# Block-causal attention with a gated convolution FFN: another static instruction order, other PSUM banks, other fill matmuls

## The chip, the cores and the metric

The kernel runs on one core of one Trainium2 chip. A time is the device time of one execution in microseconds (us). The five engines are TensorE (PE, with its weight loads as PEld), VectorE (DVE), ScalarE (ACT), GpSimd (POOL) and SyncE (SP, which here only issues transfers).

## The reference

The mask is by blocks of 64 positions; the scores are taken with q and k of 8 batches, 8 heads, 576 positions and 64 elements a head. The output of the attention goes through a two-layer network with a convolution of three taps as a gate.

```python
scores = scale * np.matmul(q, k.transpose(0, 1, 3, 2))
mask = block_i >= block_j                       # blocks of 64
scores = np.where(mask, scores, -1000000000.0)
attn = softmax(scores)                          # with 1e-09 added to the sum
x = (attn @ v).transpose(0, 2, 1, 3).reshape(8, 576, 512)
h = np.maximum(x @ w_in, 0.0)                   # 512 -> 1024
conv_out = sum(conv_w[k] * hp[:, k:k + S, :] for k in range(3))
return (h * sigmoid(conv_out)) @ w_out          # 1024 -> 512
```

## The kernel before

The work is written as 4,929 small operations, each for one engine, in a list (`Plan`, whose method `op` records them). For each there is a function that issues its instructions. `follow` then issues them in the order of a table of numbers, `ORDER`; each engine runs its own instructions in that order and waits by semaphores for what it needs from the others. Two more tables go with it: `BANKS` gives each accumulator the one of the eight PSUM banks that it lives in, and `FILLS` names operations ahead of which some matmuls without use are issued (line L1204: 128x512 matmuls into a bank that nobody holds at that moment; `32:0:12` means ahead of operation 32, into bank 0, 12 matmuls).

The attention goes by pairs of heads. For the first batch a pair is visited twice: part A is blocks 0 to 3, part B blocks 4 to 8; all later pairs are one visit. Of a visit these steps matter here, with their lines:

- loads: `qkf` (L564), `qT`, `kT` (L535), `vn` (L548), `vxa` (L574); the weights, 64-bit numbers, are `gh`, `gl` (w_in, L722) and `x` (w_out, L750). SP issues all of them, but for the first k tile and two pieces of w_in, which ACT issues.
- part A alone: PE transposes q and k (L800), ACT copies them out of PSUM (L508).
- scores: PE, L867, `banks<-kT,qT`; DVE takes the maxima (L879), PE exchanges them between halves (L888, or POOL and ACT by L503 and L842), DVE combines them (L902); ACT takes the exponentials with their sums (L911, `p`).
- DVE transposes the probabilities (L979) into `pta` (part A, two buffers) or `ptw` (all others, a single buffer); PE multiplies them by v (L990).
- DVE scales the result (L1001), ACT and POOL split it in a high and a low part (L1005, L1009).

The network of a half of a batch (`ffn`) follows when its four pairs are done: per 128 of the 1024 channels 12 matmuls (L1043), then ACT and DVE in turn (L1057, L1060, L1064, L1068, L1073, L1076, L1080) and POOL (L1083); then the products with w_out, 24 matmuls a tile (L1109), whose result ACT takes out of PSUM (L1117, `stage`) and SP stores (L1120). At the start ACT, DVE and POOL also take the weights apart into two 32-bit halves (L586 to L630), with three matmuls and one ACT copy for each piece (L685, L688, L691, L697).

Each PSUM bank is held from the first matmul that writes it to the last instruction that reads it; a PE instruction that opens a bank waits for the last reader before.

Of the kernel before, what the change touches and what calls it, by code (L numbers as in the profile page):

```python
# [184 lines left out]
"""  # L185

FILLS = """
32:0:12 30:0:13 64:0:2 69:1:2 126:0:7 235:6:4 512:2:1 250:0:6 532:0:2 390:7:3 813:0:2 4909:0:3
"""


# [1048 lines left out]
```

## Time and profile before

| | |
|---|---|
| runs shown | 670.77, 671.48 (median), 672.11 us |
| the profiled execution's own time | 671.29 us |
| its span (first to last instruction) | 669.4 us |
| busy, share of the span | PE 97%, PEld 81%, DVE 84%, ACT 80%, POOL 47% |
| granted clock of TensorE | 1.000 |
| L1204 matmuls (fills) | 57 |

The span leaves out 1.9 us of the profiled execution. A busy PE is not a PE at its peak: matmuls are pipelined, and each is shown longer than the distance to the next.

### The profile page before, as it was taken

The numbers are of one execution on the slowest core, as the hardware profiler recorded it, in microseconds if no ns is written. First come the engines' busy times: TensorE is split into PE (matmuls) and PEld (weight loads), VectorE is DVE, ScalarE is ACT, GpSimd is POOL, SyncE is SP. The second block draws the span as 40 slices with busy tenths as digits, with TensorE's granted clock in tenths as the row PEclk, the third lists the DMA queues.
The fourth block names the chain that finished last, engine by engine and source line by source line (L and its number), as shares of the span: only waits on it lengthen the run. The fifth ranks groups of instructions, "written<-read, shape, count | busy, mean of one in ns | idle before, by whom it ended". The sixth has DMA issues, their size and how long they took to land.

```text
span 669.4 us, 24942 instructions
## 1 busy us (share of the span) xinstructions
PE 652.0 (97%) x9734; PEld 544.0 (81%) x9734; DVE 560.4 (84%) x1333; ACT 537.1 (80%) x1989; POOL 315.1 (47%) x651
## 2 busy tenths in 40 slices
PE   8888999999999999999999999999999999999997
PEld 6666678768888788788888798888879798799986
DVE  3998889998999889997989779997899869995641
ACT  5998879967989786897888778997888787895643
POOL 0454455654356524446355534555555515444421
PEclk9999999999999999999999999999999999999999
DMA  7996752355454353425333442542353451230001
GB/s 176 194 215 143 145 104 50 70 105 91 73 104 96 64 97 78 99 44 103 74 72 72 97 96 41 117 90 43 75 99 79 93 92 43 48 87 1 17 32 63
DMA packets 238521, 58.26 MB, mean 87 GB/s; under 512 B 228524, under 2 KB 232900, under 8 KB 238404
## 3 DMA queue, kind: packets, MB, share of 16 engines
q1 hardware_dynamic: 237060, 55.76, 41.6%
q8 instruction: 76, 1.25, 0.8%
q10 hardware_dynamic: 1344, 0.92, 0.5%
q14 instruction: 41, 0.34, 0.2%
HBM read 47.21 MB, written 9.44 MB: 85 GB/s over the span
## 4 chain that ended last, share of the span: by engine, by line
PE 74%; DVE 4%; ACT 3%; issue 1%; POOL 0%; ACTq 0%; POOLq 0%; DVEq 0%
PE banks L1109 27%; PE banks L1043 27%; PE banks L867 11%; PE banks L990 10%; ACT p L911 1%; DVE st L879 1%; DVE ptw L979 1%; DVE t L1064 1%; DVE t L1076 1%; DVE t L1068 0%; ACT gh L1080 0%; ACT t L1073 0%; DVE rb L961 0%; DVE kT L820 0%; ACT t L1060 0%
## 5 line engine op out<-in xcount | busy, mean ns | idle before, releaser
L911 ACT ACTIVATE p<-banks,st 128x160 f32<-128x160 f32 (+8 forms) x576 | 220.9, 401 | 22.2 <-DVE st L902 20.4
L1043 PE MATMUL banks<-x,wih 128*128 128x290 f32 (+3 forms) x1024 | 185.1, 300 | 0.5 <-ACT p L911 0.4
L1043 PEld LDWEIGHTS banks<-x,wih 128*128 128x128 f32 x1024 | 154.2, 188 | 10.9 <-issue 4.5
L1083 POOL TENSOR_TENSOR gl<-t,gh 128x289 fp32r<-128x289 f32 (+3 forms) x128 | 106.1, 839 | 97.0 <-ACT gh L1080 82.4
L979 DVE STREAM_TRANSPOSE ptw<-p 128x448 f32<-128x448 f32 (+8 forms) x272 | 128.7, 498 | 13.5 <-ACT p L911 7.0
L879 DVE TENSOR_REDUCE st<-banks 128x2 f32<-128x320 f32 (+7 forms) x288 | 125.5, 472 | 11.0 <-PE banks L867 9.9
L503 POOL TENSOR_SCALAR st<-st 32x4 f32<-32x4 f32 (+2 forms) x280 | 67.7, 242 | 122.7 <-DVE st L879 50.5
L911 ACT ACTIVATION_READ_ACCUMULATOR p<-banks,st 128x1 f32 x576 | 122.8, 213 | 0.0
L1109 PE MATMUL banks<-woh,gh 128*128 128x512 f32 (+1 forms) x296 | 118.0, 399 | 0.3 <-ACT stage L1117 0.3
L1109 PE MATMUL banks<-woh,gl 128*128 128x512 f32 (+1 forms) x296 | 115.3, 390 | 0.2 <-POOL gl L1083 0.2
L1109 PE MATMUL banks<-wol,gh 128*128 128x512 f32 (+1 forms) x296 | 115.3, 390 | 0.0
L1043 PE MATMUL banks<-x,wil 128*128 128x290 f32 (+3 forms) x512 | 105.7, 299 | 0.0
L867 PE MATMUL banks<-kT,qT 64*32 64x96 f32 (+8 forms) x4464 | 100.0, 302 | 1.5 <-DVE rb L1001 0.6
L1064 DVE SCALAR_TENSOR_TENSOR t<-h,cw,t 128x289 f32<-128x289 f32 (+3 forms) x128 | 70.8, 558 | 29.0 <-ACT t L1060 28.4
L867 PEld LDWEIGHTS banks<-kT,qT 64*32 64x32 f32 x4464 | 69.7, 105 | 23.5 <-issue 4.1
L990 PEld LDWEIGHTS banks<-ptw,vn 64*64 64x64 f32 x2304 | 72.3, 133 | 20.0 <-issue 4.7
L990 PE MATMUL banks<-ptw,vn 64*64 64x160 f32 (+8 forms) x2304 | 85.2, 297 | 2.5 <-issue 1.4
L1043 PEld LDWEIGHTS banks<-x,wil 128*128 128x128 f32 x512 | 81.6, 188 | 4.3 <-issue 2.5
L1060 ACT ACTIVATE t<-h,cw 128x289 f32<-128x289 f32 (+3 forms) x128 | 68.0, 539 | 6.3 <-POOL gl L1083 2.0
L1068 DVE SCALAR_TENSOR_TENSOR t<-h,cw,t 128x288 f32<-128x288 f32 (+3 forms) x128 | 69.8, 555 | 1.4
L1073 ACT ACTIVATE t<-t 128x289 f32<-128x289 f32 (+3 forms) x128 | 55.1, 447 | 18.9 <-DVE t L1068 18.3
L1076 DVE SCALAR_TENSOR_TENSOR t<-t,h 128x289 f32<-128x289 f32 (+3 forms) x128 | 63.4, 503 | 7.6 <-ACT t L1073 6.9
(105 smaller groups left out, 812.9 us busy)
## 6 DMA issues: line engine op xcount, KB each, us to landing
vn<-in_v_dram SPq DMA_DIRECT2D x128, 144.0 KB, 3.6
out_dram<-stage SPq DMA_DIRECT2D x35, 256.0 KB, 2.6
qT<-in_q_dram SPq DMA_DIRECT2D x112, 72.0 KB, 3.2
kT<-in_k_dram SPq DMA_DIRECT2D x112, 72.0 KB, 3.1
x<-in_moe_w_out_dram SPq DMA_DIRECT2D x8, 512.0 KB, 5.2
gl<-in_moe_w_in_dram SPq DMA_DIRECT2D x4, 512.0 KB, 6.7
vxa<-in_v_dram SPq DMA_DIRECT2D x8, 128.0 KB, 5.4
gh<-in_moe_w_in_dram SPq DMA_DIRECT2D x2, 512.0 KB
```

The source lines that it names most:

```text
L867: nc.tensor.matmul(both(sb)[32 * quad:32 * quad + 32, h, o:o + w].rearrange("p (u n) -> p u n", n=32), t["q"].ap[r, 64 * b + 32 * g:64 * b ...
L879: nc.vector.tensor_reduce(out=st.ap[:, 0, c, :], in_=both(sb)[:, :, off:off + w], op=ALU.max, axis=AX.X, negate=True)
L911: nc.scalar.activation(out=pt.ap[:, h, :], in_=both(sb)[:, h, off:off + w], func=AF.Exp, bias=st.ap[:, 2, c, h:h + 1], accum_out=st.ap[:, ...
L979: nc.vector.transpose(pt.ap[:, :, b:b + rise * b + 1:rise, :], x.ap.rearrange("p h (u n) -> p h u n", n=32))
L990: nc.tensor.matmul(both(vb)[o, g, 32 * (lo - b0):32 * (b1 - b0)].rearrange("p (b n) -> p b n", n=32), vat(u, h)[r, :], pt.ap[r, h, rise * ...
L1043: nc.tensor.matmul(fb.ap[:, 0:n2], wt[:, c, fs], xs[c][xi].ap[:, x0:x0 + n2], start=(n + c - c0 == 0), stop=(n + c - c0 == 3 * NCC - 1))
L1060: nc.scalar.activation(out=t.ap[:, 0:no], in_=hb.ap[:, own:own + no], func=AF.Copy, scale=cw[:, NFC + f:NFC + f + 1])
L1064: nc.vector.scalar_tensor_tensor(out=t.ap[:, i0:no], in0=hb.ap[:, own + i0 - 1:own + no - 1], scalar=cw[:, f:f + 1], in1=t.ap[:, i0:no], o ...
L1068: nc.vector.scalar_tensor_tensor(out=t.ap[:, 0:i1], in0=hb.ap[:, own + 1:own + 1 + i1], scalar=cw[:, 2 * NFC + f:2 * NFC + f + 1], in1=t.a ...
L1076: nc.vector.scalar_tensor_tensor(out=t.ap[:, 0:no], in0=t.ap[:, 0:no], scalar=1.0, in1=hb.ap[:, own:own + no], op0=ALU.add, op1=ALU.mult)
L1083: nc.gpsimd.tensor_tensor(out=gbuf[1].ap[:, f, carry:carry + no], in0=t.ap[:, 0:no], in1=gbuf[0].ap[:, f, carry:carry + no], op=ALU.subtract)
L1109: nc.tensor.matmul(fb.ap[:, 0:cut], gbuf[a].ap[:, f, cs], w[:, f, ds], start=(f == 0 and n == 0), stop=(f == NFC - 1 and n == 2))
```

## The change

Operations, functions and buffers are the same; the three tables differ. `ORDER` has the same 4,929 numbers in another order (its first line is shown), `BANKS` differs in some tens of its digits (the first line of it is shown), and `FILLS` has 14 entries with 52 matmuls where there were 12 entries with 57.

```diff
 ORDER = """
-6 3 9 7 1 83 0 8 2 20 38 32 34 33 4 11 10 5 30 19 31 21 37 64 22 23 98 65 108 96 66 99 35 68 84 67 69 97 85 70 121 24 72 39 73 273 122 78 40 25 74 41
...
 BANKS = """
-671105723673567451675050546723014567234501236723014501230123014523014501012301234501560123012301560101450101454501012345014523014523010123012301454501
...
+640115767533627451643606674523014567234501236723014501230123014523014501012301234501560123012301560101450101454501012345014523014523010123012301454501
...
 FILLS = """
-32:0:12 30:0:13 64:0:2 69:1:2 126:0:7 235:6:4 512:2:1 250:0:6 532:0:2 390:7:3 813:0:2 4909:0:3
+32:0:14 64:0:2 69:0:4 121:1:4 126:1:2 183:6:8 136:5:2 28:4:2 193:2:3 94:0:5 532:1:3 576:4:1 578:5:1 2776:2:1
```

What this moves is seen at three places. The first is the head of the program, on SP's queue. `qkf_79` is the q tile of the first pair of heads, `qkf_81` that of the second, `qkf_87` the k tile of the second, `qkf_83` and `qkf_89` those of pairs three and four. Before:

```order
L564 DMA qkf_81<-in_q_dram 128x2x64
L564 DMA qkf_87<-in_k_dram 128x2x64
L564 DMA qkf_79<-in_q_dram 128x2x64 x2
L564 DMA qkf_87<-in_k_dram 128x2x64
L564 DMA qkf_81<-in_q_dram 128x2x64
L768 DMA t<-in_moe_conv_w_dram 24x256
L722 DMA gh<-in_moe_w_in_dram 128x2x256
```

and now:

```order
L564 DMA qkf_79<-in_q_dram 128x2x64 x2
L564 DMA qkf_83<-in_q_dram 128x4x64
L564 DMA qkf_81<-in_q_dram 128x2x64
L564 DMA qkf_87<-in_k_dram 128x2x64
L564 DMA qkf_89<-in_k_dram 128x4x64
L564 DMA qkf_83<-in_q_dram 128x4x64
L564 DMA qkf_87<-in_k_dram 128x2x64
L564 DMA qkf_81<-in_q_dram 128x2x64
L768 DMA t<-in_moe_conv_w_dram 24x256
```

The first pair's q tile went from third to first, and the first piece of w_in on this queue went behind all q and k tiles of part A. (On ACT's queue a 512 KB piece of w_in, which stood right behind the first k tile, went behind ACT's two copies of the first pair.)

At the same place PE's first rows, up to the scores of the first pair; `qkr_86` is its k tile and `qkr_80` its q tile. Before:

```order
L1204 MATMUL banks<-wol 128x512 x12
L800 MATMUL banks<-rident,qkr_86 128x128 x2
L1204 MATMUL banks<-rident 128x512 x13
L800 MATMUL banks<-rident,qkr_80 128x128 x2
L1204 MATMUL banks<-rident 128x512 x2
L867 MATMUL banks<-kT,qT 32x128 x8
```

and now:

```order
L1204 MATMUL banks<-wol 128x512 x14
L800 MATMUL banks<-rident,qkr_86 128x128 x2
L800 MATMUL banks<-rident,qkr_80 128x128 x2
L1204 MATMUL banks<-rident 128x512 x2
L867 MATMUL banks<-kT,qT 32x128 x8
```

The 13 fills between the two pairs of transposes are gone, and two more stand ahead of the first.

The second place is on DVE, at the first visit of part B, about 40 us into the program. The five rows `ptw<-p_...` are the transposes of its probabilities for blocks 8 to 4 (`p_78` to `p_74`); the PE multiplication with v waits for the last of the five. Before, the last three of them (the first two, of `p_76` and `p_75`, stand seven and five rows ahead):

```order
L979 STREAM_TRANSPOSE ptw<-p_78 128x2x9x32
L879 TENSOR_REDUCE st_756<-banks 128x2
L958 RECIPROCAL it_807<-it_807 128x10
L879 TENSOR_REDUCE st_756<-banks 128x2 x2
L597 TENSOR_SCALAR stage<-stage 128x512
L979 STREAM_TRANSPOSE ptw<-p_77 128x2x8x32
L609 SCALAR_TENSOR_TENSOR stage<-x,stage 128x512
L979 STREAM_TRANSPOSE ptw<-p_74 128x2x5x32
```

and now all five:

```order
L979 STREAM_TRANSPOSE ptw<-p_76 128x2x7x32
L1001 TENSOR_TENSOR rb<-banks,rb 128x2x128
L979 STREAM_TRANSPOSE ptw<-p_78 128x2x9x32
L820 STREAM_TRANSPOSE qT<-qT 128x320
L879 TENSOR_REDUCE st_714<-banks 128x2
L979 STREAM_TRANSPOSE ptw<-p_74 128x2x5x32
L958 RECIPROCAL it_797<-it_797 128x10
L979 STREAM_TRANSPOSE ptw<-p_77 128x2x8x32
L879 TENSOR_REDUCE st_714<-banks 128x2
L979 STREAM_TRANSPOSE ptw<-p_75 128x2x6x32
```

The two instructions that take a piece of w_out apart (L597, L609), a piece of w_in's (L613) and the transpose of `kT` (L820) no longer stand between them.

The third place is near the end, on PE, where the first matmuls of 256 columns stand (the last tile of the output is done in two halves, in banks that held other results). Before:

```order
L1109 MATMUL banks<-woh,gh 128x512
L1109 MATMUL banks<-wol,gh 128x512
L1109 MATMUL banks<-woh,gl 128x512
L1043 MATMUL banks<-x,wih 128x290 x2
L1204 MATMUL banks<-rident 128x512 x3
L1109 MATMUL banks<-woh,gh 128x256
L1109 MATMUL banks<-wol,gh 128x256
```

and now:

```order
L1109 MATMUL banks<-woh,gl 128x512
L1043 MATMUL banks<-x,wil 128x290 x2
L1043 MATMUL banks<-x,wih 128x290 x2
L1109 MATMUL banks<-woh,gh 128x256
L1109 MATMUL banks<-wol,gh 128x256
L1109 MATMUL banks<-woh,gl 128x256
```

The three fills are gone. The bank that this half opens (bank 5 in both) was last read by an ACT copy of a finished tile (L1117). That copy stood between the last gate instructions on ACT, directly ahead of this half:

```order
L1080 ACTIVATE gh<-t 128x289
L1073 ACTIVATE t<-t 128x289
L1080 ACTIVATE gh<-t 128x289
L1117 ACTIVATE stage<-banks 128x512
L1080 ACTIVATE gh<-t 128x289
```

and now stands, as one of two, well ahead of them:

```order
L1060 ACTIVATE t<-h,cw 128x289
L1073 ACTIVATE t<-t 128x289 x3
L1117 ACTIVATE stage<-banks 128x512 x2
L1080 ACTIVATE gh<-t 128x289 x2
L1073 ACTIVATE t<-t 128x289
```

with two tiles taken out in a row.

## Rows read from the trace of the kernel before

**Rows 1.** Busy time of the engines in stretches of the span: start and end, length, then for PE, PEld, DVE, ACT and POOL the busy us and the number of instructions, the granted clock, the share of time that the transfer engines were busy, GB/s.

```profile
0.00:20.00 20.00, 17.79 (x286) 13.80 (x293) 9.04 (x39) 12.53 (x51) 2.79 (x10) 1.00 0.78 184
20.00:40.00 20.00, 17.21 (x383) 11.75 (x366) 18.70 (x61) 19.01 (x77) 8.77 (x12) 1.00 0.96 202
40.00:60.00 20.00, 17.68 (x273) 13.07 (x270) 17.61 (x44) 17.78 (x52) 11.29 (x14) 1.00 0.98 197
60.00:100.00 40.00, 37.10 (x603) 27.27 (x602) 34.42 (x81) 32.83 (x97) 18.68 (x25) 1.00 0.62 116
100.00:160.00 60.00, 56.47 (x883) 44.92 (x885) 56.64 (x128) 49.70 (x203) 31.66 (x71) 1.00 0.47 86
160.00:600.00 440.00, 439.86 (x6902) 374.78 (x6893) 391.72 (x920) 369.18 (x1424) 217.88 (x487) 1.00 0.40 79
600.00:640.00 40.00, 40.00 (x296) 35.96 (x295) 24.50 (x51) 23.98 (x65) 16.07 (x24) 1.00 0.02 8
640.00:669.40 29.40, 25.86 (x151) 22.50 (x149) 7.80 (x15) 12.07 (x29) 7.94 (x10) 1.00 0.15 54
```

**Rows 2.** The chain of work that ended last, pieces of it: start, length, engine and line, number of instructions.

```profile
126.55 1.88 DVE ptw L979 x6
...
142.62 2.64 ACT p L911 x16
...
158.88 2.81 PE banks L990 x65
...
264.38 11.44 PE banks L1109 x48
...
391.58 12.00 PE banks L1043 x90
```

**Rows 3.** The fills, out of PE's instructions grouped by line and names: shape, count, busy us, mean ns of one (to its modelled end), idle time ahead of them and what ended it.

```profile
L1204 PE MATMUL banks<-rident 128*128 128x512 f32 x45 | 12.7, 406 | 0.4 <-DVE it L934 0.4
...
L1204 PE MATMUL banks<-wol 128*128 128x512 f32 x12 | 4.7, 566 | 1.1 <-DVE wol L497 1.1
```

**Rows 4.** Instructions in order of time at the head: start, length, engine, line, names, shapes, count, and in brackets the idle time before it and what ended it.

```profile
0.74 0.44 SPq L564 DMA_DIRECT2D qkf<-in_q_dram  x1
...
1.13 4.69 PE L1204 MATMUL banks<-wol 128*128 128x512 f32 x12 [1.13 <-DVE wol L497]
...
1.74 0.97 SPq L564 DMA_DIRECT2D qkf<-in_q_dram  x2
1.78 0.49 ACTq L722 DMA_DIRECT2D gh<-in_moe_w_in_dram  x1
...
5.66 0.29 PE L800 MATMUL banks<-rident,qkr 128*128 128x128 f32 x2
...
5.79 3.23 PE L1204 MATMUL banks<-rident 128*128 128x512 f32 x13
5.98 0.38 ACT L508 ACTIVATE kT<-banks 128x256 f32<-128x256 f32 x1 [1.14 <-PE banks L800]
...
8.85 0.29 PE L800 MATMUL banks<-rident,qkr 128*128 128x128 f32 x2
...
9.18 0.38 ACT L508 ACTIVATE qT<-banks 128x256 f32<-128x256 f32 x1 [2.81 <-PE banks L800]
...
9.62 0.96 PE L867 MATMUL banks<-kT,qT 64*32 64x128 f32 x64
...
12.18 0.94 PE L867 MATMUL banks<-kT,qT 64*32 64x128 f32 x64 [0.20 <-ACT qT L508]
12.23 0.37 ACT L911 ACTIVATE p<-banks,st 128x128 f32<-128x128 f32 x1
```

**Rows 5.** Transfers by tile: queue, count, KB each, median us from issue to landing.

```profile
qkf<-in_q_dram SPq DMA_DIRECT2D x4, 64.0 KB, 4.2
...
qkf<-in_k_dram ACTq DMA_DIRECT2D x2, 64.0 KB, 2.4
```

**Rows 6.** DVE in order of time at the first visit of part B, from the first transpose of its probabilities to the last (columns as in rows 4).

```profile
39.72 0.65 DVE L979 STREAM_TRANSPOSE ptw<-p 128x448 f32<-128x448 f32 x1 [0.51 <-ACT p L911]
40.28 0.40 DVE L613 TENSOR_SCALAR gl<-gl 128x512 int32<-128x512 int32 x1
...
41.13 0.49 DVE L820 STREAM_TRANSPOSE kT<-kT 128x320 f32<-128x320 f32 x1
...
44.24 0.41 DVE L597 TENSOR_SCALAR stage<-stage 128x512 int32<-128x512 int32 x1
...
45.20 0.65 DVE L609 SCALAR_TENSOR_TENSOR stage<-x,stage 128x512 int32<-128x512 int32 x1
45.77 0.50 DVE L979 STREAM_TRANSPOSE ptw<-p 128x320 f32<-128x320 f32 x1
```

**Rows 7.** PE and ACT in order of time near the end (columns as in rows 4).

```profile
651.77 0.43 PE L1043 MATMUL banks<-x,wih 128*128 128x290 f32 x2
...
652.04 0.86 PE L1204 MATMUL banks<-rident 128*128 128x512 f32 x3
...
652.53 0.58 ACT L1117 ACTIVATE stage<-banks 128x512 f32<-128x512 f32 x1
...
653.16 0.39 PE L1109 MATMUL banks<-woh,gh 128*128 128x256 f32 x1 [0.26 <-ACT stage L1117]
```

**Rows 8.** PE's waits over the whole span: who waited for whom, us in total, times, longest us.

```profile
PE banks L990 <- DVE ptw L979: 1.0, 2, 0.7
```

More of the change, by code (lines that the diff above doesn't have):

```diff
@@ L19 @@
 ORDER = """
[158 rows of a table removed]
[158 rows of a table added]
 """
 BANKS = """
-671105723673567451675050546723014567234501236723014501230123014523014501012301234501560123012301560101450101454501012345014523014523010123012301454501
-450101014523012301450123014523015623012323450145450101456723012301014523014536561467450167674501234567564556452323674523454545234523452345454567236745
-236745424665476236663232747564465374320726524576776456264474566455337637721054645435763402457104102376722604156601463204322043747674763766776236767676
-6737671504652
+640115767533627451643606674523014567234501236723014501230123014523014501012301234501560123012301560101450101454501012345014523014523010123012301454501
+450101014523012301450123014523015623012323450145450101456723012301014523014536561324450167674501234567564545452323674523454545234523452345454567236745
+236745244565476266763232747564566227341726452776676456573470566455327623766475645735462743457104712176742624156601643204027471747674763766776236767676
+6737671506052
 """
 FILLS = """
-32:0:12 30:0:13 64:0:2 69:1:2 126:0:7 235:6:4 512:2:1 250:0:6 532:0:2 390:7:3 813:0:2 4909:0:3
+32:0:14 64:0:2 69:0:4 121:1:4 126:1:2 183:6:8 136:5:2 28:4:2 193:2:3 94:0:5 532:1:3 576:4:1 578:5:1 2776:2:1
 """
```

315 rows, old and new, of the table ORDER are left out of this document.

## The prediction

> **What bounds the kernel now.** I began with the busy time by stretches [rows 1]. In it one should look at PE and DVE together. Between 160 and 640 us PE is never idle (479.86 of 480 us). Before 160 us it is idle 13.8 us (160 less 17.79, 17.21, 17.68, 37.10 and 56.47), and there DVE is the fullest engine, 56.64 of the 60 us from 100 to 160. After 640 us PE stops 3.5 us before the end, for the last copy and store. So 160 us is a border: ahead of it DVE and ACT hold PE up, behind it PE alone counts. The chain of work that ended last says the same [rows 2]: until 158.88 us its pieces are DVE's and ACT's (six transposes in 1.88 us, sixteen exponentials in 2.64 us), from there on PE's, one stretch after the other. In these stretches PE runs at its pace: 48 matmuls of L1109 in 11.44 us are 0.238 us each, 90 of L1043 in 12.00 us are 0.133 us each, and the mean granted clock is 1.00. A different order of the same matmuls can't shorten 160 to 640 us; it can only add waits there. What may be won lies in two places, the head, where every us by which DVE and ACT are ahead at 160 us comes off the end, and the tail.
>
> Busy hides something at the head. The fills count as busy, though they compute nothing. They are 57, 45 in 12.7 us and the first 12 in 4.7 us [rows 3], nearly all of them ahead of 160 us. Idle time and fills together are some 30 us of PE in the head. A fill that stands where PE would wait costs nothing, and one that stands ahead of ready work costs 0.235 us.
>
> **The head, term by term.** The first scores of before start at 9.62 us [rows 4]. The q tile's transposes run at 8.85 us, right behind 13 fills that started at 5.79 us. 3.06 us for 13 is 0.235 us each. ACT copies q out at 9.18 us after 2.81 us of idling, and the scores follow when that copy ends. In the new order k's and q's transposes stand side by side. Two more fills ahead of them shift k's from 5.66 us to 5.66 + 2 x 0.235 = 6.13 us. ACT's copy of k began 0.32 us behind its transposes and took 0.38 us, so 6.45 to 6.83 us; that of q follows, to 7.21 us; the scores start at about 7.2 us. That is 2.4 us sooner, if q has landed by 6.1 us. It is now first in SP's queue, so issued at 0.74 us and about 0.5 us later; tiles of this kind took 2.4 us from ACT's queue and 4.2 us on SP [rows 5], so it lands by 5.5 us at the latest. The first exponential came 12.23 - 9.62 = 2.61 us behind the scores, so it can come at 9.8 us: for ACT, which had done little but copies by then, a gain of up to 2.4 us.
>
> The second pair gets less of it. Its scores started at 12.18 us, when ACT had copied its q and k [rows 4]. In the new order two exponentials stand ahead of these two copies. 9.8 us, two exponentials at 0.37 us and two copies at 0.38 us give 11.3 us, 0.9 us sooner. So at this point DVE and ACT have a lead of 0.9 to 2.4 us, and I take **1.5 us**, nearer to the lower end because DVE needs the second pair's scores to stay full.
>
> Does the lead last to 160 us? From 20 to 160 us DVE is busy 127.4 of 140 us and ACT 119.3 [rows 1], so a lead of 1.5 us can be kept, and it can be eaten by any wait in those 12.6 us of DVE's idle time. One place where DVE's order speaks for keeping it is the first visit of part B. Its five transposes took from 39.72 to 45.77 + 0.50 = 46.27 us [rows 6], with other work in between that the multiplication by v doesn't need: pieces of the weights (0.40, 0.41 and 0.65 us) and `kT` (0.49 us), 1.95 us together, which now stand elsewhere. DVE must still do them, so this is no gain of its own; it brings forward what PE waits for, and is a reason why PE can use the lead. I count it at nothing, with 1 us as its upper bound (half of the 1.95).
>
> **The tail.** Before, PE ends its last but one piece of L1043 at about 652.04 us, issues three fills, and then waits for ACT's copy L1117, which started at 652.53 us; the half tile begins at 653.16 us [rows 7]. From 652.04 to 653.16 us are 1.12 us in which PE does nothing of use, and behind it there is only PE work to the end. In the new order the fills are gone and that copy stands well ahead of the last gate instructions. The gain is between nothing (the copy is late in another way) and 1.12 us; I take **1.1 us**.
>
> **The other fills.** 54 stood ahead of the tail, and now 52. Up to the scores of the fourth pair there are 40 and 38. They stand where PE waits anyway, as PE's idle time there shows, so I count the difference at nothing; were it all on the path, it would be 2 x 0.235 = 0.5 us.
>
> **The banks.** No instruction is added for them. Where a bank's last reader is late, PE waits as in the tail; I count nothing outside it.
>
> **Sum.** 1.5 + 1.1 = 2.6 us off. The profiled execution took 671.29 us, so 668.7 us. Its time lies 0.2 us under the median of the runs shown, 671.48, so for a median I say **668.9 us**.
>
> **Rivals.**
>
> *The lead is lost on the way.* The transfer engines are 96 and 98% busy from 20 to 60 us [rows 1]. If DVE and ACT come sooner to pieces of weights and tiles that land no sooner, they wait, and only the tail's gain is left: 671.5 - 1.1 = 670.4 us. For it speaks that the first 512 KB piece of w_in goes from 1.78 us to behind ACT's copies, some 7 us. Against it, that in before DVE and ACT were themselves nearly full in that stretch. The Trainium skill (DMA: Bandwidth & Descriptors, Issuing engines are not separate DMA queues) says that transfers of all issuing engines run on the same 16 DMA engines and interleave; by it, moving that piece off ACT's queue frees the way for q and k, and pays later. Rows 5 fit it, with 2.4 us for the first tiles and 4.2 us for those issued around the large piece. By it this rival would weigh less, some 0.2. As tiles and weights both have to land before 60 us whatever their order, it keeps a chance of 0.25.
>
> *More than that.* The whole 2.4 us reaches 160 us, and the part B visit gives its 1 us: 671.5 - 1.1 - 2.4 - 1.0 = 667.0 us. Chance 0.13.
>
> *PE's clock falls at the head.* The first 12 matmuls took from 1.13 to 5.66 us, 0.378 us each on average, against 0.235 us from 5.79 us on [rows 4], so part of them ran at the lower of two levels, 1.2 against 2.4 GHz. PE had up to then done nothing. The Trainium skill (TensorE: Matmul & The Clock Gate, Part 1) says that the slow clock is the default and that activity releases it. By it a head with 16 fills ahead of the first scores in place of 27 could lose the clock again. A second stretch like the first costs 12 x (0.378 - 0.235) = 1.7 us, which leaves 668.9 + 1.7 = 670.6 us. Against it: in both orders fills stand between the first steps (2, 4, 4 and 2 of them), and in before no granted clock under 1.00 is shown in any stretch. Chance 0.04.
>
> *Slower: new waits where PE had none.* From 160 to 600 us PE has 24 visits to serve. If in the new order PE reaches the multiplication by v ahead of DVE's last transpose, each such wait goes straight into the time, as nothing there is idle. In before this wait occurred twice, 0.7 us the longest [rows 8], both in the head. Eight of them would be 8 x 0.7 = 5.6 us, and the time 668.9 + 5.6 = 674.5 us. It decides from (2.6 + 1.3) / 0.7, so six of 24 visits, on. Against it: summing PE's rows at their durations, these multiplications stand at the same amount of PE work in both orders, to within 2 us, and DVE is at 89% in this stretch. Chance 0.12.
>
> *Nothing changes.* The gain at the head is lost, and at the tail a bank waits elsewhere: 671.3 us, chance 0.04. What is left, 0.42, is my forecast.
>
> **From the cases to the numbers.** A measurement of this kernel can tell 0.2%, which is 1.3 us, so from 670.1 us down it is faster and from 672.8 us up it is slower. Of my forecast 0.38 falls under 670.1 us (a lead of 0.3 us is enough with the tail's 1.1 us), of the first rival 0.07, of the second all: 0.58. Slower is nearly all of the fourth, 0.11. The rest is 0.31. For the range I leave out the slower rival (0.12) and the outer part of the second: 666.6 to 672.0 us. The likeliest case alone runs from 667.6 to 670.2 us (a lead of 2.4 or of 0.4 us, and the tail).
>
> **What would show it.** Right: the first scores near 7.2 us and the first exponential near 9.8 us; the fourth pair's scores about a us sooner than before; the chain passing to PE for good some 1.5 us of idle time and fills earlier; no gap of PE between the last L1043 and the first 256-column matmul. Wrong: DVE or ACT waiting for a transfer between 20 and 60 us, PE idle in a stretch after 160 us, a granted clock under 1.00 behind 5 us, or the head's idle time and fills unchanged although the first scores come sooner.

## The result, and the profile after

The changed kernel took 676.68 us (median of 5 runs, 675.34 to 678.36) beside 671.92 us for the kernel before: a ratio of 1.0071 [1.0046, 1.0096]. It is slower, by 0.7%; I had said 668.9 us. Its profiled execution took 675.53 us (span 673.7 us), 4.2 us more than that of before. Two executions among the experiments below, of 1038 us (tail_early) and 1596 us (pe_old), lie far from all others and are left out of the times there.

The busy time by stretches of the kernel after (columns as in [rows 1]):

```profile
0.00:20.00 20.00, 17.33 (x277) 13.07 (x277) 9.14 (x41) 12.17 (x53) 3.35 (x10) 1.00 0.81 179
...
100.00:160.00 60.00, 58.34 (x909) 47.13 (x911) 55.63 (x133) 51.30 (x207) 34.25 (x76) 1.00 0.50 88
160.00:600.00 440.00, 437.29 (x6856) 370.60 (x6849) 385.64 (x906) 365.21 (x1399) 218.16 (x481) 1.00 0.39 78
600.00:640.00 40.00, 39.45 (x299) 35.65 (x298) 24.94 (x53) 25.57 (x79) 16.35 (x25) 1.00 0.12 34
```

From 160 to 600 us PE is now idle 2.7 us, where it was idle 0.14 us, and 46 matmuls fewer fall into it. Which waits those are is seen in PE's waits between 160 and 600 us (who waited for whom, us in total, times, longest):

```profile
PE banks L867 <- ACT p L911: 1.3, 3, 0.5
PE banks L1043 <- DVE rb L1001: 0.4, 1, 0.4
PE banks L1043 <- ACT stage L1117: 0.3, 1, 0.3
PE banks L1043 <- ACT h L1057: 0.2, 1, 0.2
PE banks L867 <- ACT h L1057: 0.2, 1, 0.2
```

In the kernel before this list is empty. None of the five is a wait for an input: scores and L1043 do not read `p`, `rb`, `stage` or `h`. They open a PSUM bank, and wait for the last reader of what the bank held before. One of them in order of time (columns as in [rows 4]): it is step 3096 of the list, which opens bank 3 behind the same reader in both kernels. First in the kernel after:

```profile
435.66 0.54 PE L1043 MATMUL banks<-x,wih 128*128 128x290 f32 x2
...
436.10 0.27 DVE L958 RECIPROCAL it<-it 128x18 f32<-128x18 f32 x1
...
437.10 0.42 DVE L1076 SCALAR_TENSOR_TENSOR t<-t,h 128x289 f32<-128x289 f32 x1
...
437.44 0.75 DVE L1001 TENSOR_TENSOR rb<-banks,rb 128x576 f32<-128x576 f32 x1
...
438.24 0.54 PE L1043 MATMUL banks<-x,wih 128*128 128x290 f32 x2 [0.45 <-DVE rb L1001]
```

and the same steps in the kernel before:

```profile
432.26 0.54 PE L1043 MATMUL banks<-x,wih 128*128 128x290 f32 x2
...
433.40 0.72 DVE L1001 TENSOR_TENSOR rb<-banks,rb 128x576 f32<-128x576 f32 x1
...
435.84 0.43 PE L1043 MATMUL banks<-x,wih 128*128 128x290 f32 x2
```

Before, DVE was done with the bank at 434.12 us and PE opened it again 1.7 us later. Now DVE's reciprocal stands later and a gate product (L1076) ahead of the normalising product L1001, which ends at 438.19 us; PE comes to the bank earlier in its own order (2.6 us behind its first step shown, not 3.6), stops, and starts 0.05 us behind that end.

Idle time understates this, as a matmul's modelled end covers part of a wait. So I compare by progress: PE's matmul steps, without the fills, are the same in all kernels here. I give each kind the distance from start to start that it usually has (0.118 us for a matmul of 256 columns, 0.235 us for one of 512, and so on), sum them in each kernel's order, and read when each kernel starts the step at which a given sum is reached. The differences to the profiled execution of before, in us (plus is later):

| kernel (profiled execution) | at 107 us of matmul work (154 us) | at 200 (250 us) | at 300 (352 us) | at 400 (453 us) | at 560 (617 us) | at the end |
|---|---|---|---|---|---|---|
| after | -1.2 | +0.5 | +1.5 | +4.4 | +5.4 | +4.1 |

The whole loss, 6.6 us, is made between 154 and 617 us, bit by bit, the largest part of it (2.9 us) between 352 and 453 us. Head and tail are a little better than before. Each row of this kind is one execution, and the head alone scatters by 1 us or more.

The head came as forecast for its first steps and then lost its lead (after, in order of time, answering [rows 4]):

```profile
1.13 4.82 PE L1204 MATMUL banks<-wol 128*128 128x512 f32 x14 [1.13 <-DVE wol L497]
...
5.78 0.45 PE L800 MATMUL banks<-rident,qkr 128*128 128x128 f32 x4
...
6.82 0.94 PE L867 MATMUL banks<-kT,qT 64*32 64x128 f32 x64
...
9.50 0.34 ACT L911 ACTIVATE p<-banks,st 128x96 f32<-128x96 f32 x1 [1.76 <-DVE st L902]
...
10.88 0.95 PE L867 MATMUL banks<-kT,qT 64*32 64x128 f32 x64
...
12.90 0.43 ACT L586 ACTIVATE gh<-gh 128x256 f32<-128x256 f32 x1 [1.23 <-DMA gh<-in_moe_w_in_dram]
...
14.62 0.29 PE L930 MATMUL banks<-st,same 64*64 64x4 f32 x6 [1.20 <-ACT p L911]
...
21.16 0.94 PE L867 MATMUL banks<-kX,qT 64*32 64x128 f32 x64 [0.24 <-ACT kX L508]
```

The last row is the scores of the fourth pair. In the kernel before they are

```profile
19.75 0.95 PE L867 MATMUL banks<-kX,qT 64*32 64x128 f32 x64 [0.43 <-ACT qT L508]
```

At the tail the half tile follows PE's L1043 with no gap (answering [rows 7]):

```profile
652.54 0.43 PE L1043 MATMUL banks<-x,wih 128*128 128x290 f32 x2
652.81 0.28 PE L1109 MATMUL banks<-woh,gh 128*128 128x256 f32 x1
```

### The profile page after: what moved, and what is told of

It reads as the page before. It is cut to its first block, busy times and chain, and to the rows that moved or that the text cites. A ratio compares the mean times of both kernels' runs of the same rounds, so it can differ in the third digit from the quotient of the medians.

```text
span 673.7 us, 24935 instructions
## 1 busy us (share of the span) xinstructions
PE 654.7 (97%) x9729; PEld 543.3 (81%) x9729; DVE 559.6 (83%) x1333; ACT 539.0 (80%) x1989; POOL 320.1 (48%) x651
## 5 line engine op out<-in xcount | busy, mean ns | idle before, releaser
L1043 PE MATMUL banks<-x,wih 128*128 128x290 f32 (+3 forms) x1024 | 189.5, 301 | 1.1 <-DVE rb L1001 0.4
L1043 PEld LDWEIGHTS banks<-x,wih 128*128 128x128 f32 x1024 | 155.4, 188 | 14.4 <-issue 5.5
L879 DVE TENSOR_REDUCE st<-banks 128x2 f32<-128x192 f32 (+8 forms) x288 | 125.2, 474 | 21.3 <-PE banks L867 18.1
L979 DVE STREAM_TRANSPOSE ptw<-p 128x64 f32<-128x64 f32 (+8 forms) x272 | 127.3, 498 | 13.8 <-ACT p L911 6.0
L503 POOL TENSOR_SCALAR st<-st 32x10 f32<-32x10 f32 (+2 forms) x280 | 69.8, 249 | 128.2 <-DVE st L879 53.7
L1043 PE MATMUL banks<-x,wil 128*128 128x290 f32 (+3 forms) x512 | 106.3, 297 | 0.0
L867 PE MATMUL banks<-kT,qT 64*32 64x96 f32 (+8 forms) x4464 | 101.6, 302 | 1.9 <-ACT p L911 1.3
L867 PEld LDWEIGHTS banks<-kT,qT 64*32 64x32 f32 x4464 | 71.2, 105 | 24.9 <-issue 5.9
L1064 DVE SCALAR_TENSOR_TENSOR t<-h,cw,t 128x286 f32<-128x286 f32 (+3 forms) x128 | 69.5, 549 | 24.1 <-ACT t L1060 23.6
L1043 PEld LDWEIGHTS banks<-x,wil 128*128 128x128 f32 x512 | 82.3, 188 | 3.3 <-issue 1.1
L1068 DVE SCALAR_TENSOR_TENSOR t<-h,cw,t 128x287 f32<-128x287 f32 (+3 forms) x128 | 70.4, 557 | 1.5
L1076 DVE SCALAR_TENSOR_TENSOR t<-t,h 128x289 f32<-128x289 f32 (+3 forms) x128 | 62.6, 498 | 9.7 <-ACT t L1073 9.0
```

The source lines that it names most:

```text
L503: nc.gpsimd.tensor_scalar(out=dst, in0=src, scalar1=1.0, scalar2=0.0, op0=ALU.mult, op1=ALU.add)
L867: nc.tensor.matmul(both(sb)[32 * quad:32 * quad + 32, h, o:o + w].rearrange("p (u n) -> p u n", n=32), t["q"].ap[r, 64 * b + 32 * g:64 * b ...
L879: nc.vector.tensor_reduce(out=st.ap[:, 0, c, :], in_=both(sb)[:, :, off:off + w], op=ALU.max, axis=AX.X, negate=True)
L979: nc.vector.transpose(pt.ap[:, :, b:b + rise * b + 1:rise, :], x.ap.rearrange("p h (u n) -> p h u n", n=32))
L1043: nc.tensor.matmul(fb.ap[:, 0:n2], wt[:, c, fs], xs[c][xi].ap[:, x0:x0 + n2], start=(n + c - c0 == 0), stop=(n + c - c0 == 3 * NCC - 1))
L1064: nc.vector.scalar_tensor_tensor(out=t.ap[:, i0:no], in0=hb.ap[:, own + i0 - 1:own + no - 1], scalar=cw[:, f:f + 1], in1=t.ap[:, i0:no], o ...
```

## The experiments

All times are medians of 5 to 12 executions. Ratios are to the kernel before, run beside each on the same chip; they are worked out from all these executions and can differ a little from the ratio of two medians. "Progress" is the comparison explained above, for the one profiled execution of each kernel.

### Which stretch loses: splices of the two orders

The orders differ so little at any point (some five of the steps issued so far) that one can begin with one and end with the other. The step numbers give `ORDER`; `BANKS` and `FILLS` follow the order from which a bank or a step comes.

```diff
-ORDER, BANKS, FILLS of one kernel
+head_new:  first 1107 steps of the new order, the others as before
+head_old:  first 1115 steps as before, the others of the new order
+tail_new:  first 4867 steps as before, the others of the new order
+both_ends: head_new up to its step 4867, the others of the new order
+tail_609:  first 4629 steps as before, the others of the new order
```

> The new order, its banks and fills up to the point where PE has issued 107 us of its matmul work (about 156 us into the span), the order before from there to the end. Theory: the time is lost by the new order in the steady stretch itself, where the two traces drift apart by 6.5 us between 156 and 640 us; the new head is worth 1.1 us there (PE reaches this point at 1.1 us earlier in the trace after). Then this kernel takes about 670.8 us against 671.9 before. Rival: the steady stretch is slow because of what the new head hands on to it (a PE that runs ahead of ACT and DVE, other loads in flight). Then it takes about 676 us, like the changed kernel.

> The complement: the order before up to the point where PE has issued 108 us of its matmul work (about 157 us), the new order from there to the end. Theory (loss made by the new order in the steady stretch): 676.7 + 1.1 = about 677.8 us. Rival (loss handed on by the new head): 671.9 - 1.2 (the new tail) = about 670.7 us.

> The order before up to the point where PE has issued 593 us of its matmul work (about 650 us), the new tail from there: the copy of the second-last output stage moved ahead and three fills gone. My tail term said 1.1 us; the drift of the two traces over this stretch is 1.2 us. Theory: about 670.7 us. Rival: the tail's gain in the changed kernel was only PE catching up on a wait that had been paid for before, and is not to be had here: 671.9 us, the time before.

> New head up to 107 us of matmul work, the order before in the middle, new tail from 593 us on. If the stretches are independent (theory): 671.9 - 1.1 - 1.2 = about 669.6 us, faster than both kernels. If the new head makes the middle slow (rival): about 675 us.

> The order before up to 551 us of PE's matmul work (about 607 us of the span), the new order from there to the end. The first splice of the tail was cut inside the last block's output multiplication and made waits of its own. Theory (the tail term of the prediction, 1.1 us; in the trace after PE makes up 1.2 us over this stretch): 671.7 - 1.2 = about 670.5 us. Rival (PE only catches up what the steady stretch had lost): 671.7 us.

| kernel | us | ratio | progress at 107, at 560, at the end |
|---|---|---|---|
| head_new | 672.18 | 1.0003 [0.9992, 1.0013] | -1.0, -0.1, -0.1 |
| head_old | 675.77 | 1.0049 [1.0032, 1.0066] | +1.6, +6.7, +5.4 |
| tail_new | 672.24 | 0.9998 [0.9983, 1.0013] | -0.8, -0.8, -0.6 |
| both_ends | 671.89 | 1.0003 [0.9993, 1.0014] | -1.2, +0.4, +0.5 |
| tail_609 | 670.50 | 0.9981 [0.9963, 0.9998] | +0.4, +0.3, -1.0 |

The steady stretch loses whatever the head: 5.1 us in head_old, with much the same list of waits, against 0.9 us in head_new (its lead, given back by 189 us for the most part), whose list between 160 and 600 us is empty. So most of the loss is not handed on by the head, and head_new's rival has fallen. Whether a smaller part is, stays open: head_old's profiled execution took 676.48 us, while four others with a mean granted clock of 0.999 or 1.000 took 673.6 to 674.1 us, under the 675.3 and 675.5 us of the changed kernel. The new head is worth nothing that the median shows. Its lead of 1.0 us at 154 us is 0.3 us at 189 us, when the order before goes on behind it; and the same old head stood at -0.8, +0.4 and +1.6 us at this point in three executions, so 1 us is within its scatter.

The tail is worth 1.3 us, but only from 607 us on: 0.3 to -1.0 in tail_609, and 1.3 us in every kernel here that has the new order from there. The splice at 650 us cut through the last output products and won nothing (-0.8 to -0.6 and +0.4 to +0.5), so my expectation of it was wrong. **tail_609 beats both kernels**, the kernel before by 0.19%; the upper end of that interval is close to no change.

### The two edits that the tail term named

```diff
-... 4889 4890 4842 4891 4843 4859 4844 4880 4763 4860 4845 4764 4909 ...
+... 4889 4890 4763 4764 4842 4891 4843 4859 4844 4880 4860 4845 4909 ...
-... 813:0:2 4909:0:3
+... 813:0:2
```

> The kernel before with just the two edits that the prediction's tail term named: the copy of the finished tile (L1117, and its store) is placed five steps of ACT earlier, and the three fills ahead of the half tile are gone. Theory (the tail term of 1.1 us is these two edits): 672 - 1.1 = about 670.8 us, and PE goes from its last piece of L1043 to the half tile without a gap. Rival (the gain that the new order makes behind 607 us comes from its whole order there): under half a us, since the copy, put ahead of the gate instructions, makes those late and PE waits for them instead.

671.54 us, ratio 0.9994 [0.9978, 1.0009], no change that the times can tell; by progress 0.6 us won, between theory and rival. (The copy, step 4763, is moved ahead of two steps of ACT, 4843 and 4859, not five as I had written.) The gap ahead of the half tile is closed, and a part of it opens again six us later. PE's weight loads between 650 and 668 us:

```profile
PEld banks L1109 <- POOL gl L1083: 0.6, 1, 0.6
PEld banks L1109 <- ACT gh L1080: 0.4, 1, 0.4
```

PE arrives earlier at products whose inputs come no earlier. So by progress about half of the tail's 1.3 us are the two edits, and the rest belongs to the order around them.

### Bank numbers, or the order

```diff
 ORDER, FILLS as in the kernel after
-BANKS: those of the kernel after
+BANKS: from 158 to 645 us the bank out of use for longest, by the trace after (199 digits differ)
```

> The changed kernel in its own order, with other bank numbers between 158 and 645 us: each bank object that is opened there gets, of the banks free at that place of the order, the one whose last reader ended longest ago in the trace after (the whole choice made together, two-bank tiles kept adjacent). 199 of 463 numbers change. In the order as it stands only 2 to 4 banks are free at most of the tight openings, so the openings less than 0.1 us behind a reader fall from 31 to 25 only. Theory (the order leaves no older bank): at most 1 us is won, 675.7 to 676.7 us. Rival (the numbers in the table of banks are badly chosen): the 5 us come back, about 672 us.

674.57 us, ratio 1.0043 [1.0026, 1.0061]. By progress it loses 4.7 us between 154 and 617 us, the kernel after 6.6 us. So some 2 of 6.6 us were the numbers in the table of banks, more than I expected, and the rest remains: the scores still wait for `p` three times, 1.3 us in all.

### Repairing single waits

late_open puts PE's waiting step behind others; early_rel puts the releasing step of ACT or DVE ahead of others (on the bank numbers of rebank); tail_early does the latter to the stalls of tail_609. One of eight, nine and six places each (step 3096 is the opening at 438.24 us; 1623 is an exponential, 1388 a ReLU; 1069 a normalising product):

```diff
 late_open
-3328 3139 3389 3096 3372 3086 3329 3376 3469 3087 3371 3140
+3328 3139 3389 3372 3086 3329 3376 3469 3087 3371 3140 3096
 early_rel
-1372 1388 1362 1406 1619 1323 1620 1345 1363 1621 1373 1622 1651 1674 1623
+1619 1620 1621 1622 1623 1361 1654 1344 1372 1388 1362 1406 1323 1345 1363 1373
 tail_early
-1051 1091 1092 822 1130 1081 1072 1069
+1051 1069 1088 1079 1080 1090 1091 1092 822
```

> The changed kernel with eight steps of PE moved, and nothing else: at eight places between 205 and 601 us where its trace shows PE waiting to write into a bank that ACT or DVE is still reading, the waiting matmul step is issued behind the next one to four steps of PE that do not depend on it. The time lost ahead of these eight openings in the trace after sums to 3.7 us, of which about 0.7 us (two openings by the output multiplication) is lost in the trace before too. Theory (PE reaches reopened banks too early; each wait is its own loss): 676.7 - 3.0 = about 673.7 us, and the eight waits gone from the trace. Rival (ACT and DVE are behind by their own amount of work, and PE's waits only show it): the waits turn up at the next openings, and the time stays at about 676.7 us.

> The changed kernel with the new bank numbers of the earlier run (674.6 us), and at nine of its waits between 206 and 600 us the step that gives the bank free (an exponential, a ReLU or the normalising multiplication that reads it last) is placed ahead of the one to three steps of ACT or DVE that stood before it in the queue; PE's order is unchanged. The nine stalls sum to 3.7 us. Theory (the loss is releases queued too late on ACT and DVE): 674.6 - 3 = about 671.5 us, the nine waits gone. Rival (ACT and DVE lack time there, so that whatever is put behind is late for PE next): 674 to 675 us.

> The order before with the new tail (670.5 us) and the same treatment at six of its own stalls between 133 and 463 us (2.4 us in sum): the step of ACT or DVE that gives the bank free is placed ahead of one or two others. Theory (late releases): 670.5 - 1.5 = about 669 us. Rival (the stalls stand there because the engines have no time to spare): 670.5 us.

late_open took 675.30 us (1.0054 [1.0034, 1.0075]); by progress it loses 6.3 us where the kernel after loses 6.6. Moved openings no longer wait, and others do; the rival was nearer. early_rel got worse by 3.6 us (678.17 us, 1.0092 [1.0072, 1.0113]) and tail_early by 3.8 us (674.28 us, 1.0041 [1.0025, 1.0057]). In early_rel the wait at 214 us is gone, and 10 us later stands a longer one. PE's step there, and PE's stretches around it:

```profile
224.35 3.04 PE L867 MATMUL banks<-kT,qT 64*32 64x160 f32 x112 [2.05 <-ACT p L911]
```

```profile
220.00:224.00 4.00, 2.31 (x72) 1.89 (x64) 3.16 (x10) 3.56 (x15) 1.72 (x6) 1.00 0.04 10
224.00:228.00 4.00, 3.65 (x114) 2.79 (x115) 3.82 (x9) 2.87 (x10) 2.64 (x3) 0.70 0.94 175
228.00:232.00 4.00, 4.00 (x17) 3.22 (x16) 3.64 (x9) 2.92 (x16) 2.04 (x5) 0.88 0.76 160
```

What was overtaken there (a ReLU and the first scaling of the gate, which DVE's gate products need) came later itself; that this is how the next exponentials got late is my reading, and no run shows it alone. As PE's order is the same in rebank and early_rel, each matmul can be compared with itself: early_rel is 0.8 us later at 205 us, 0.2 us at 213 us, where the wait is gone, and 3.1 us at 230 us. From there to 590 us the distance stays within 0.3 us, and at 615 us it is 3.8 us. So the loss was made at two places, above all this one, and the moves between them brought nothing, though rebank's longer waits there (0.5 us at 297 us the longest) were gone. Part of the loss at the first place is the granted clock of the stretches shown, 0.70 and 0.88: 4 x 0.30 + 4 x 0.12 = 1.7 us by estimate. So the theory of late releases is wrong here; the rival was nearer, but put the cost too low.

### A square: PE's order against the order of the others

Between 178 and 612 us the two orders can be mixed by engine. The bank numbers there had to be chosen anew for this, by one rule for all four; it judged how long a bank was out of use from the list of steps, with all steps of ACT, DVE and POOL set ten places ahead.

```diff
 between step 1300 and 552 us of matmul work, in the changed kernel:
+all_new: PE new,       others new,      new bank numbers
+pe_old:  PE as before, others new,      new bank numbers
+pe_new:  PE new,       others as before, new bank numbers
+all_old: PE as before, others as before, new bank numbers
```

> First of four kernels that form a square. All four have the changed kernel's head up to 129 us of matmul work (about 178 us of the span) and its tail from 552 us of matmul work (about 612 us); in between, PE's steps stand in one of the two orders and the steps of DVE, ACT, POOL and SP in one of the two, and all bank numbers in between are chosen anew by one rule (a bank as long out of use as can be had). Here PE and the others have the new order. Theory P (PE's new order reaches banks and inputs too early): 674.5 us, as the kernel with new bank numbers alone had. Theory Q (the new order of DVE, ACT and POOL releases too late): the same, 674.5 us. It is the base for the next three.

> The square: PE in the order before, DVE, ACT, POOL and SP in the new order. Theory P (it is PE's order): about 671 us, like the kernel with all in the order before. Theory Q (it is the order of the engines that release the banks): about 674.5 us, like the kernel with all in the new order. Theory I (each order fits only its own partner): over 676 us.

> The square: PE in the new order, DVE, ACT, POOL and SP in the order before. Theory P: about 674.5 us. Theory Q: about 671 us. Theory I: over 676 us.

> The square: all engines in the order before between 178 and 612 us, with new bank numbers there, between the new head and the new tail. If stretches are independent: the kernel before less the new tail's 1.2 us and less the 0.1 to 0.3 us that the new head is worth, about 670.4 us. If bank numbers matter by themselves in the order before too: another 0.5 us up or down.

> New head to 107 us of matmul work, the order before to 551 us, the new tail from there, all with the bank numbers of their own tables. Theory (stretches independent; the new head worth 0.1 us at the end, the new tail 1.2 us): 670.4 us, beside the 687 us of the same order with bank numbers by the rule. Rival (the 16 us of the square came from somewhere else than the bank numbers): over 680 us.

best_a has almost the stretches of all_old, with the tables' own bank numbers; six of its twelve executions had the lower clock of the next section.

| kernel | us | ratio |
|---|---|---|
| all_new | 687.45 | 1.0235 [1.0202, 1.0267] |
| all_old | 686.95 | 1.0221 [1.0195, 1.0247] |
| pe_old | 714.44 | 1.0638 [1.0604, 1.0671] |
| pe_new | 713.72 | 1.0619 [1.0590, 1.0649] |
| best_a | 670.37 | 0.9997 [0.9980, 1.0013] |

Theories P and Q had said 670 to 675 us for the square, only theory I (for the mixtures) over 676. One thing follows clearly: bank numbers alone are worth 16.6 us here (all_old against best_a). all_old waits between 180 and 620 us, first of all,

```profile
PE banks L867 <- DVE rb L1001: 3.7, 4, 0.9
PE banks L990 <- ACT p L911: 3.0, 3, 1.3
PE banks L867 <- ACT p L911: 2.2, 3, 1.2
```

as I read it because the rule took banks for free that ACT and DVE give back later than the list says. Either mixture costs 26 to 28 us more, so P and Q fall, and theory I's sign came. But its cause is not shown: each of the four has bank numbers of its own by the same rule, and what the mixtures wait for is again the last reader of a bank, as in pe_old:

```profile
PE banks L867 <- DVE rb L1001: 8.4, 6, 2.0
PE banks L867 <- ACT h L1057: 5.9, 5, 3.3
PE banks L1043 <- ACT h L1057: 3.3, 2, 1.8
```

Whether a mixture with well chosen numbers would be slow too, no run tells. Part of the difference is TensorE's clock: the mean granted clock of the mixtures' executions is 0.985 to 0.993, so by estimate up to (1 - 0.985) x 712 = 10.7 us of pe_old. With bank numbers this bad, the two unmixed orders cost the same, so the square doesn't tell which engine's order makes the 4.7 us that rebank still loses.

### The head: a load, fills and the clock

```diff
 head_win (on head_new): step 83, a load of w_in on ACT's queue
-... 32 30 33 31 38 83 64 ...
+7 1 0 6 83 4 2 ...
 head_fill (on head_new)
+79:0:5
 few_fills (on the kernel before)
-32:0:12 30:0:13 64:0:2
+32:0:12 64:0:2
```

> The kernel with the new head and the order before from 156 us on, with one step moved: the first load of the input weights (ACT's queue, first half of the first tile) is issued at the start, as in the kernel before, and not at 6.9 us. In the trace after ACT waits 1.2 us for this load at 12.9 us, with the exponentials of the third pair of scores behind it, and PE waits 1.7 us for these. Theory (the lead of the first scores is lost on this load): PE is 1.2 us earlier than with the new head alone where it has issued 5 us of matmul work, and about 0.5 to 1.2 us of it is left at the end: about 671.2 us against 672.2. Rival (the loads between 20 and 60 us take the lead, whatever came ahead of them): the early gain is there and gone by 100 us of matmul work, 672 us.

> The new head with the order before from 156 us on (672.2 us; five of its twelve executions had a mean granted clock of 0.997 and took 673.0 us, the others 671.1 to 671.4 us), with five fill matmuls more, placed where PE waits 0.9 us for the exponentials at 14.2 us. Theory (with fewer fills the granted clock falls for about 2 us near 16 us in part of the executions): the clock stays up in nearly all executions, and the median is about 671.4 us. Rival (the lower clock has nothing to do with fills): again some four in ten executions at 0.997, 672 us or, by the five fills' 1.2 us less the wait they cover, 672.4 us.

> The kernel before with its group of 13 fills ahead of the first q transpose taken out, nothing else. Theory (fills hold the clock): the clock falls near the head in most executions, the mean clock is 0.997 or less in them, and the median about 673.5 us instead of 671.6. Rival: the fills stand in idle time of PE and nothing hangs on them, 671.6 us.

head_win: 673.12 us, 1.0018 [1.0004, 1.0032]; it settles nothing on the load. ACT's wait is still there, 1.23 us at 13.21 us: the piece it waits for (128x256) comes by SP's queue, where it is issued at 9.24 us, behind all q and k tiles (at 7.43 us in the kernel after), and I had moved the other one.

What it showed was something else. Its mean granted clock was 0.997 or less in 10 of 12 executions, and in its trace one sees where (columns as in [rows 1]):

```profile
12.00:16.00 4.00, 2.61 (x68) 2.03 (x62) 2.64 (x11) 2.79 (x15) 0.46 (x1) 0.87 0.56 116
16.00:20.00 4.00, 4.00 (x62) 3.13 (x47) 2.05 (x11) 2.24 (x11) 1.23 (x2) 0.71 0.99 198
```

PE waits, is busy 2.61 of 4 us, and for a part of these two stretches (granted clock 0.87 and 0.71) runs at the lower of the two levels, 1.2 in place of 2.4 GHz. Over all runs the kernel before had a mean clock of 0.997 or less in 18 of 140 executions, which took 673.7 us in the median, and the others 671.6 us: such a fall costs 2.1 us. The changed kernel had it in 3 of 5 executions, 676.7 to 678.4 us beside 675.3 and 675.5 us. So about 1 us of the 4.8 us between the medians is the clock; the two executions without a fall lie 3.8 us over the 671.6 us. No trace shows where the falls of the changed kernel stand. Nor does a median show all that the new head and tail are worth: best_a's six executions without a fall took 670.1 us in the median, 1.5 us under the kernel before beside it (671.6 us, no fall in 23). With the new head the fall comes more often (6 of 12 in best_a, 5 of 12 in head_new), and gives back a part of what is won.

few_fills: 673.67 us, 1.0018 [1.0002, 1.0033], with the lower clock in 8 of 12 executions (6 of 23 of the kernel before beside it). In its trace:

```profile
16.00:20.00 4.00, 3.06 (x86) 2.30 (x84) 2.15 (x8) 3.68 (x17) 0.97 (x3) 1.00 0.79 196
20.00:24.00 4.00, 3.09 (x49) 1.61 (x57) 3.31 (x15) 3.38 (x19) 1.25 (x2) 0.57 1.14 184
```

The 13 fills stood in idle time, and taking them out makes the fall more frequent and the kernel slower, by little (the interval almost reaches no change). head_fill: 672.31 us, 1.0003 [0.9990, 1.0017], the lower clock in 5 of 12 as without its five fills (head_new's seven others took 670.9 to 672.6 us, not 671.1 to 671.4 as I had written); in its profiled execution the clock fell near 96 us instead. So its theory is not borne out. Which of the waits in the new head matters is open.

## Why the prediction was wrong

**What bounds the kernel** was right, and so was its warning: a different order can only add waits between 160 and 640 us. **The step that failed is "The banks": "I count nothing outside it".** By progress the stretch behind 154 us added 6.6 us, up to the tail. I had the mechanism in hand, the tail's wait for L1117, and didn't ask at each reopening of a bank how far its last reader stood behind. The slower rival named this stretch, and its time, 674.5 us, came near, but by another wait: for DVE's transposes ahead of the multiplication by v, which [rows 8] had shown. Between 160 and 600 us no such wait occurred. So that its time came near is luck. Its counter-argument, that the multiplications stand at the same amount of PE work in both orders, compared PE with PE. At step 3096 what counted was how far DVE's last reading of the bank stood ahead of PE: 1.7 us in the order before, nothing in the new one.

**The head.** First scores at 6.82 us (I said 7.2), first exponential at 9.50 (9.8), second pair's scores at 10.88 (11.3): right, with some luck in the size. The 14 fills ahead of k's transposes took hardly longer (1.13 to 5.78 us) than the 12 of before (1.13 to 5.66 us), as the fills' distance fell from 0.43 to 0.23 us at 4.2 us in this execution and at 4.7 us in before's; in head_new, with the same head, the first scores came at 7.86 us. "I take 1.5 us" as what reaches 160 us was wrong: the fourth pair's scores start at 21.16 us, 1.4 us later than before (19.75), and nothing measurable is left in head_new. That is the first rival, the lead lost on the way, though in part earlier than its 20 to 60 us. What took it is shown only in part: the wait for the piece of w_in at 12.9 us and the 1.2 us of PE behind it. In head_new this wait is 0.44 us, and the fourth pair's scores are as late (21.49 us). Part B's transposes and the fills, counted at nothing, can't be told from the head's scatter.

**The clock** at the head was a rival with 0.04 and 1.7 us. A fall occurred in three of five executions, at some 2.1 us each; where, no trace of this kernel shows. In head_win, with the same head but for one load, it stands at 12 to 20 us behind a wait of PE, where I had looked only for a second cold start. So 0.04 was too small. The Trainium skill (TensorE: Matmul & The Clock Gate, Part 1) says that the fast clock depends on activity; few_fills agrees, with 8 of 12 executions against 6 of 23.

**The tail.** 1.1 us forecast, 1.3 us measured; the two edits I gave as its cause account for 0.6 us, so the size is partly luck.

**Sums.** Leads of 2.4 and 0.4 us with the tail give 668.0 and 670.0 us, not 667.6 and 670.2. The 3.5 us of idle time after 640 us hold the 0.26 us of the tail's gap; PE ends 3.3 us before the end.

**Open** is which steps make the 4.7 us that remain with better bank numbers: no repair of single waits brought it back, in either direction. That the loss lies in waits at reopened banks is shown by the traces, and for some 2 us by rebank; for the rest no run has removed it and left the order in place.

## What to carry to other kernels

Where a static order has an engine that never waits, a new order is judged by its distances between the last reader of each bank and the next opening, on the engines' real times; position in a list doesn't tell, and a badly chosen bank table can cost more than the new order did (16.6 us here, against 4.8 us). Moving the step that ends a wait ahead of others on a nearly full engine didn't help in either of two kernels: in the one followed step by step, one move put a wait of 2.05 us in place of one of 0.54 us, and most others changed nothing. Splicing two orders at a few points finds the stretch that gains and keeps it.

## What the runs showed of the hardware that I had not expected

A wait of PE can cost twice: early_rel's 2.05 us at 224 us is followed by a stretch with a granted clock of 0.70 and one of 0.88, in the midst of the steady stretch. Executions of one and the same kernel with and without such a fall lie 2.1 us apart, more than the head and the tail of this change together.
